# Regrouping a filter's DFT units beside the first batch of an MLP mixer: three places a step, and a thinner row of the second half

## The chip, the cores and the metric

The kernel runs on one core of a Trainium2 chip. The metric is the time of one execution in microseconds of that core. Engines: PE is TensorE, DVE is VectorE, ACT is ScalarE, POOL is GpSimd, SP is the queue that issues most loads. The granted clock (PEclk in the profiles) is the share of TensorE's full speed that was granted, as the profile records it; "half clock" below means matmuls that take up to twice as long where this figure is low: in the profile of the kernel before, two matmuls of L398 took 1.91 us at 355.92 (granted clock 0.50 from 356 to 359 us) and 1.02 us at 363.59 (1.00 from 360 to 370 us).

## The reference, cut to what matters

```python
# x: (8, 3008, 256) fp32
X = np.fft.rfft(x, axis=1)
Y = X * (filt_r + 1j * filt_i)[None]
x = np.fft.irfft(Y, n=3008, axis=1)                       # the filter
h = np.maximum(x.transpose(0, 2, 1) @ w_tok1, 0) @ w_tok2 # token mixing
u = x + h.transpose(0, 2, 1)
out = u + np.maximum(u @ w_ch1, 0) @ w_ch2                # channel mixing
```

The length 3008 is split as 64 x 47. For every batch the filter is 12 "length-64 units" (one matrix multiplication each) and, for a group of one or two batches, 32 "length-47 units" (a multiplication, the complex product with the filter on VectorE, and a multiplication back). A bank is the buffer in PSUM that such a multiplication writes; the next unit that uses the same bank has to wait until it has been read (for the length-64 units TensorE waited 16.7 us in all for this in the first profile of the kernel before).

## The kernel before

The batches go in the groups (0), (1, 2), (3, 4), (5, 6), (7). While the mixer works on one group, the filter of the next runs beside it, as a generator whose next step is called at fixed places of the mixer. Beside the first batch the last ten weights are converted too. (Code below is cut: `...` and missing arguments stand for what is left out.)

```python
def a_unit(b, c, tag):                      # length-64 unit
    ps = bank(tag)                          # beside the mixer: the one bank "b"
    nc.tensor.matmul(ps, wa, xs.pop((b, c))...)
    t1 = t1p.tile(...)
    nc.scalar.copy(out=t1, in_=ps)          # frees the bank
    nc.scalar.dma_start(z_d..., t1)

def dft(bs):
    ...
    for i, u in enumerate(todo):            # 24 length-64 units for two batches
        a_unit(*u, ("acc", "b")[i % 2] if first else "b")
        if i + XB < len(todo):
            x_load(*todo[i + XB])           # XB = 2: two x tiles
        yield
    ...
    load(0); load(1)
    yield
    yield
    for k in range(K2 + 1):                 # length-47 units, K2 = 32
        if k < K2:
            b_unit(k)                       # matmul to bank "b", four DVE operations
            ...
        if k >= 1:
            bi_unit(k - 1)                  # matmul to bank "acc", ACT copy
        yield
```

One step of the mixer (36 steps a batch: six blocks of rows, m, times six pairs of hidden tiles, jp); the yields are the places where the filter gets its turn:

```python
for i in range(n + 1):
    now, old = i < n, i >= 1
    next(convert, None)                     # first conversion: an ACT copy, five DVE operations
    if now:
        ...
        s = up_first(jp, ...)               # 8 matmuls, ACT copy
        up_middle(hhs[i], w, g, s)          # DVE
    one_step()                              # DVE: a piece of a finished block, or sums for the next
    if old:
        for f in h_sums(...): f()           # DVE
        down(mo, jo, 0, ...)                # 6 matmuls
    next(convert, None)                     # second conversion
    if now:
        up_last(jp, ...)                    # 6 matmuls, 2 DVE sums, 2 ACT relus
    one_step()
    loads()
    yield                                   # (1)
    if old:
        down(mo, jo, 1, ...)                # 8 matmuls
        if jo == JP - 1:
            todo_v.extend(finish(...))      # the block's finish: DVE
            one_step(); one_step()
    if now:
        if m + 1 < MT and jp in (3, 4):
            u_part(b, m + 1, jp - 3)        # token part: 12 matmuls, only in steps 3 and 4 of six
            ...
    loads()
    yield                                   # (2)
```

```python
for i, _ in enumerate(mix(b, next_ready, convert)):
    if not done and i % len(bs) == 0:       # first batch: at every yield; pairs: at (1)
        done = next(todo, "end") == "end"
```

## Time and profile before

| | |
|---|---|
| time, median | 2670.48 us (2663.97 to 2670.58, 3 runs) at first; 2668.18 us (4 runs) with the rounds of the change |
| first up-projection of the mixer | 202.31 us |
| second batch's first up-projection | 603.92 us |
| steps 0 to 4 (with conversions) | 75.47 us |
| steps 5 to 12 (rest of the length-64 units) | 67.83 us |
| steps 13 to 29 (length-47 units) | 195.17 us |

A step's start is read off TensorE's timeline: the first of the eight matmuls of line L492, the up-projection. Its length is the distance to the next one. How the page and the windows are read is shown in the prediction, on the lines themselves.

### The profile page before, as it was taken

How to read it: one execution, taken by the hardware profiler on the slowest of the kernel's cores; microseconds unless marked ns; L12 is line 12 of the kernel's file. 1: busy time of each engine (PE TensorE's matmuls, PEld its weight loads, DVE VectorE, ACT ScalarE, POOL GpSimd, SP SyncE). 2: the span in 40 equal slices, each digit the busy share in tenths (PEclk: the TensorE clock that was granted, in tenths of full speed). 3: DMA queues.
4: the chain of work that ended last, by engine and by line, in shares of the span. 5: the costliest groups of instructions: out<-in, count | busy, mean ns of one | idle time of the engine just before them, and what ended most of it. 6: DMA issues, size and time to landing. Idle time of an engine off the chain costs nothing.

```text
span 2667.9 us, 31511 instructions
## 1 busy us (share of the span) xinstructions
PE 2511.5 (94%) x10840; PEld 1997.6 (75%) x10840; DVE 1825.9 (68%) x3505; ACT 677.4 (25%) x1325; POOL 503.4 (19%) x926
## 2 busy tenths in 40 slices
PE   4666999999999999999999999999999999999997
PEld 1344766687787777788877777788888888888886
DVE  3886588846567688745658588755678586647675
ACT  2222322212322222212322122222222122212221
POOL 2324211111212111121121112121121111211221
PEclk8778999999999999999999999999999999999999
DMA  8663344322332222212233223211322211100000
GB/s 219 190 188 111 114 119 122 96 77 79 96 103 83 72 78 75 70 32 63 90 99 89 66 84 85 79 33 41 103 70 79 55 46 56 24 9 8 17 15 17
DMA packets 167158, 210.28 MB, mean 79 GB/s; under 512 B 35868, under 2 KB 115633, under 8 KB 166998
## 3 DMA queue, kind: packets, MB, share of 16 engines
q1 hardware_dynamic: 92937, 111.56, 14.4%
q0 software_dynamic: 30976, 44.53, 6.9%
q10 hardware_dynamic: 43085, 52.17, 6.0%
q8 instruction: 86, 1.41, 0.2%
q14 instruction: 74, 0.61, 0.1%
HBM read 133.15 MB, written 74.97 MB: 78 GB/s over the span
## 4 chain that ended last, share of the span: by engine, by line
PE 71%; DVE 16%; issue 2%; ACT 2%; DMA 0%; SPq 0%; DVEq 0%; POOL 0%; ACTq 0%; POOLq 0%
PE ps_po L526 24%; PE ps_pg L492 14%; PE ps_pg L508 11%; PE ps_acc L452 6%; PE ps_acc L435 5%; DVE t L470 3%; PE ps_acc L457 3%; DVE hh L470 3%; PE ps_b L382 2%; PE ps_b L349 2%; PE ps_acc L398 2%; DVE u L470 2%; DVE s L470 2%; DVE p L392 1%; DVE p L391 1%
## 5 line engine op out<-in xcount | busy, mean ns | idle before, releaser
L470 DVE TENSOR_TENSOR hh<-ps_pg,s 128x512 f32<-128x512 f32 (+3 forms) x864 | 482.6, 586 | 639.7 <-ACT s L495 639.7
L571 POOL DMA_DIRECT2D out_dram<-r x757 | 409.7, 550 | 1971.5 <-ACT hh L513 855.6
L513 ACT ACTIVATE hh<-hh 128x512 f32<-128x512 f32 (+1 forms) x576 | 347.9, 621 | 1141.6 <-DVE hh L470 1141.6
L526 PE MATMUL ps_po<-t,wc 128*128 128x256 f32 (+1 forms) x2304 | 535.8, 375 | 3.7 <-DVE t L470 2.4
L526 PEld LDWEIGHTS ps_po<-t,wc 128*128 128x128 f32 x2304 | 434.4, 190 | 128.3 <-issue 50.4
L492 PE MATMUL ps_pg<-v,wc 128*128 128x256 f32 (+1 forms) x1728 | 417.5, 378 | 1.5 <-DVE v L470 1.5
L526 PE MATMUL ps_po<-hh,wc 128*128 128x256 f32 (+1 forms) x1728 | 413.3, 375 | 3.1 <-ACT hh L513 3.1
L492 PEld LDWEIGHTS ps_pg<-v,wc 128*128 128x128 f32 x1728 | 330.5, 192 | 42.5 <-DVE v L470 1.9
L526 PEld LDWEIGHTS ps_po<-hh,wc 128*128 128x128 f32 x1728 | 328.2, 190 | 42.2 <-ACT hh L513 5.1
L508 PE MATMUL ps_pg<-u,wc 128*128 128x256 f32 (+1 forms) x1152 | 294.3, 378 | 16.0 <-DVE hh L470 15.7
L470 DVE TENSOR_TENSOR t<-t,hh 128x256 f32<-128x256 f32 (+1 forms) x576 | 243.5, 423 | 19.8
L508 PEld LDWEIGHTS ps_pg<-u,wc 128*128 128x128 f32 x1152 | 215.3, 190 | 52.8 <-DVE hh L470 28.6
L470 DVE TENSOR_TENSOR s<-ps_pg,hh 128x512 f32<-128x512 f32 (+1 forms) x288 | 196.1, 681 | 30.0
L452 PE MATMUL ps_acc<-w,h 128*128 128x512 f32 (+1 forms) x384 | 181.7, 596 | 15.8 <-ACT h L441 11.6
L470 DVE TENSOR_TENSOR t<-hh 128x512 f32<-128x512 f32 (+1 forms) x288 | 193.1, 671 | 0.6 <-ACT hh L513 0.6
L435 PE MATMUL ps_acc<-t,w 128*128 128x256 f32 x768 | 169.5, 383 | 6.3 <-DMA t<-g_tmp 5.0
L492 PE MATMUL ps_pg<-u,wc 128*128 128x256 f32 (+1 forms) x576 | 172.4, 381 | 0.4 <-DVE hh L470 0.4
L398 PE MATMUL ps_acc<-p,wi 128*96 128x512 f32 (+1 forms) x320 | 148.2, 546 | 23.7 <-DVE p L393 12.3
L508 PE MATMUL ps_pg<-v,wc 128*128 128x256 f32 (+1 forms) x576 | 169.2, 375 | 0.0
L435 PEld LDWEIGHTS ps_acc<-t,w 128*128 128x128 f32 x768 | 147.1, 192 | 28.1 <-issue 5.8
L382 PE MATMUL ps_b<-t,wb 96*128 96x512 f32 (+1 forms) x288 | 132.7, 542 | 23.2 <-DVE p L392 11.4
L495 ACT COPY s<-ps_pg 128x256 f32<-128x256 f32 (+1 forms) x288 | 105.8, 367 | 148.6 <-PE ps_pg L492 144.5
(67 smaller groups left out, 1947.5 us busy)
## 6 DMA issues: line engine op xcount, KB each, us to landing
z_tmp<-t ACTq DMA_DIRECT2D x96, 256.0 KB
t<-z_tmp SPq DMA_DIRECT2D x128, 192.0 KB
g_tmp<-t ACTq DMA_DIRECT2D x128, 192.0 KB
t<-g_tmp SPq DMA_DIRECT2D x48, 512.0 KB
x<-in_x_dram SPq DMA_DIRECT2D x184, 128.0 KB
out_dram<-r POOLq DMA_DIRECT2D x698, 32.0 KB, 1.8
wb<-wb_t SPq DMA_DIRECT2D x80, 96.0 KB
wi<-wi_t SPq DMA_DIRECT2D x80, 96.0 KB
```

The costliest lines, as they stand in the source:

```text
L382: nc.tensor.matmul(ps, wbs[k // WC][:, k % WC, :], t2s[k // KC][:, k % KC], start=True, stop=True)
L398: nc.tensor.matmul(ps[0:KR], wis[k // WC][:, k % WC, :], prods.pop(k), start=True, stop=True)
L435: nc.tensor.matmul(acc[:, t, :], w1[:, a, ts(t, P)], t4[b, a // TC4][:, a % TC4, :], start=(a == 0 and t == 0), stop=(a == A - 1 and t == ...
L452: nc.tensor.matmul(ps[:, 0:w], h1[:, t, ts(dh, P)], w2[:, t, ds(m * 512, w)], start=(t == 0), stop=False)
L457: nc.tensor.matmul(ps[:, ds(q * P, n)], t4[b, c][:, r, ts(dh, P)], wai[:, 0:n], start=False, stop=(q == 3))
L470: nc.vector.tensor_tensor(out=out, in0=in0, in1=in1, op=op)
L492: nc.tensor.matmul(ps[:, 0:hw], wc1[:, jp, n, :], mov, start=True, stop=True)
L495: nc.scalar.copy(out=s[:, 0], in_=g[0][:, 0, 0:hw])
L508: nc.tensor.matmul(ps[:, 0:hw], wc1[:, jp, n, :], mov, start=True, stop=True)
L513: nc.scalar.activation(out=hs, in_=hs, func=AF.Relu)
L526: nc.tensor.matmul(po[i][:, j, 0:hw], wc2[:, jp, n, :], mov, start=(jp == 0 and first == 1), stop=(jp == JP - 1 and last == 1))
L571: q.dma_start(rows[g, e, :, ds(h * A + 4 * m, n)], blocks[ts(g, CW), h, e, 0:n])
```

## The change

The intent: in the first batch's early steps TensorE idles (23.5 of 75.5 us), so give it more length-64 units there (three a step instead of two), and use the steps that this frees to take the length-47 units less densely, because VectorE is nearly full beside them (85% busy).

```diff
@@ dft
-            yield
+            yield i + 1 < len(todo)          # true until the last length-64 unit
@@ mix
                 down(mo, jo, 0, ...)
+            yield i, 0
             next(convert, None)
...
-            yield
+            yield i, 1
...
-            yield
+            yield i, 2
@@ the loop over the groups
+            spread = True
...
-                for i, _ in enumerate(mix(b, next_ready, convert)):
-                    if not done and i % len(bs) == 0:
-                        done = next(todo, "end") == "end"
+                for i, place in mix(b, next_ready, convert):
+                    if not done and (place == 1 or bs == GROUPS[0] and (spread or place == 2 and i % 3)):
+                        spread = next(todo, "end")
+                        done = spread == "end"
```

For the other groups the calls stay where they were: at place 1 of each step.

Two words for what follows. Places 0, 1 and 2 of a step are its three yields; the place of a step *in six* is its number modulo six, which is jp (step 17 is at place 5 of six). "The spread" is the second half of the change, the length-47 units taken less densely; the variable `spread` in the code is true until it begins.

## The prediction

> **What bounds the kernel now.** I read the page first, then windows cut at the stages of the first batch, then that stretch's timelines of TensorE, VectorE and ScalarE, then its waits.
>
> ```profile
> PE 2511.5 (94%) x10840; PEld 1997.6 (75%) x10840; DVE 1825.9 (68%) x3505; ACT 677.4 (25%) x1325; POOL 503.4 (19%) x926
> ...
> PE   4666999999999999999999999999999999999997
> ```
>
> TensorE is busy from the fourth slice (200 us) to the end, so its queue sets the time. The first 200 us (first group's filter, alone) are not touched. The change acts only beside the first batch of the mixer, from the first up-projection at 202.31 us to the second batch's at 603.92. I cut that stretch where TensorE's timeline shows the stages change:
>
> ```profile
> core 0: us, PE busy (x) PEld busy (x) DVE busy (x) ACT busy (x) POOL busy (x), PEclk, DMA share, GB/s
> 202.31:277.78 75.47, 51.94 (x172) 34.61 (x171) 52.40 (x91) 20.12 (x37) 31.04 (x53) 0.89 0.33 102
> 277.78:345.61 67.83, 66.66 (x278) 50.83 (x277) 38.12 (x73) 22.20 (x42) 8.73 (x16) 1.00 0.43 136
> 345.61:540.78 195.17, 181.21 (x677) 123.80 (x676) 166.64 (x286) 47.87 (x92) 25.98 (x48) 0.97 0.37 105
> 540.78:603.92 63.14, 61.55 (x303) 55.45 (x302) 28.80 (x60) 11.72 (x25) 8.65 (x16) 1.00 0.26 82
> ```
>
> Row 1 is mixer steps 0 to 4, beside which the last ten weight conversions run (two a step): TensorE is idle for 23.5 of 75.5 us. Row 2 is steps 5 to 12, with the rest of the 24 length-64 units at two a step: 1.2 us idle. Row 3 is steps 13 to 29, with the 32 length-47 units, two a step: 14.0 us idle, VectorE at 85%. Row 4 has no filter work. So the whole idle time that any regrouping here can win is 40 us, 1.5% of the time; 2% can't come from it.
>
> In row 1 TensorE isn't the bound. Its long waits are for a length-64 unit's bank, which ScalarE frees late:
>
> ```profile
> 214.67 1.12 PE L349 MATMUL ps_b<-x,wa 128*128 128x512 f32 x2 [2.66 <-ACT t L351]
> ...
> 230.74 2.08 PE L349 MATMUL ps_b<-x,wa 128*128 128x512 f32 x2 [5.21 <-ACT t L351]
> ...
> 245.85 1.40 PE L349 MATMUL ps_b<-x,wa 128*128 128x512 f32 x2 [3.55 <-ACT t L351]
> ```
>
> That copy (L351) stands in ScalarE's queue behind the relus, and these behind VectorE's conversions. VectorE in turn waits for ScalarE's first conversion copy of the next step:
>
> ```profile
> 217.68 0.43 DVE L220 TENSOR_SCALAR top<-top 128x512 uint32<-128x512 uint32 x1 [4.20 <-ACT top L219]
> ...
> 234.70 0.43 DVE L220 TENSOR_SCALAR top<-top 128x512 uint32<-128x512 uint32 x1 [5.15 <-ACT top L219]
> ```
>
> The loop of a step is therefore: relu, copy of the unit after the up-projection, the unit at the step's end on TensorE, its copy, its store's issue, conversion copy, some 11 us of VectorE work, relu. TensorE has slack beside it.
>
> In row 3 TensorE waits for VectorE to finish reading the one bank of the length-47 products:
>
> ```profile
> 497.21 1.12 PE L382 MATMUL ps_b<-t,wb 96*128 96x512 f32 x2 [1.78 <-DVE p L392]
> ```
>
> [...] ScalarE takes the conversion copy at 216.99 only after the two unit copies and the store's issue at 216.45.[...] after the 2.23 us stall at 354.90 the granted clock of 350 to 360 is 0.83, but after the 1.78 us stall at 497.21 it stays 1.00.[...] the four operations of a length-47 unit take 684, 693, 684 and 693 ns, 2.75 us in all.[...] x loads and z stores there never fill a stage (share 0.33 and 0.43).
>
> **The change part by part.** No instruction is added or removed; units move. Units per plain step on TensorE: 6.04 us mixer (step 12, with no unit), 0.86 a length-64 unit (two 512-column matmuls, 6.90 minus 6.04 in the second batch), 0.86 each for the two halves of a length-47 unit, 2.6 for the token part (L452 1.72 plus L457 0.89) in two steps of six.
>
> *Length-64 units.* Three places a step: 24 units take steps 0 to 7 instead of 0 to 11. The new place is after the first part of the down-projection, ahead of the second conversion. In steps 0 to 4 it puts five more units, 5 x 0.86 = 4.3 us, into TensorE's slack; the other steps lose as much. Does it lengthen the loop? The new unit's copy (0.58) and store issue (0.35) come ahead of the second conversion copy (0.67) on ScalarE. For step 1: down-projection ends near 220.5, unit 221.4, copy 222.0, issue 222.4, conversion copy 223.1; VectorE asks for it at 224.7. Step 2: 240.2 against 240.33. So it fits, with nothing to spare in one step: 0. In steps 5 to 7 bank b must be free between the new place and the next: six matmuls (1.29) against a copy of 0.6: it fits. The stalls of about 0.28 at the step's end occur in three steps instead of five (5, 7, 8, 11 and the one at 338.60): 0.6 gained. Sum: 4.9 us off. The x data of the third unit must arrive within one unit, 1.29, one unit and 1.73 of matmuls, 3.9 us after the first; at 286.28 a load is issued and its burst ends near 289.2, 3.0 us. It fits narrowly.
>
> *Length-47 units.* They start at step 9 and take 5 places in 3 steps, ending at step 29 as before (the last call is at step 29's middle instead of its end). The second place is left out in every third step: 0 and 3 of each six. Step lengths of before, by place in six (steps 23 to 28): 11.25, 9.91, 12.78, 11.10, 11.88, 11.88 (the last two 12.14 in the earlier, wider blocks). By work alone a plain step with two units is 9.5, so stalls are at 5, 1 and 2. At place 3, 1.73 of pure work goes: 10.4. At place 0 the same goes: 7.8. At place 1 the VectorE queue decides: the finish of a block (2.2 us) and the two products must pass. I run it through with the durations above: without the product of place 0's end, VectorE is ready for the next step at 487.2 instead of 489.95, the step begins at 484.1, its second product's bank is freed 7.2 us later (as at 347.64 to 354.84) at 494.4, so the step is 12.3, still stalled. Places 2 and 5 keep their queues: 11.1 and 11.25. So the stalls stay, and the units now spend stalls in one more step (11). Steps 8 to 29: 6.0+9.5+12.1+11.25, then twice 7.8+12.3+11.1+10.4+12.1+11.25, then 7.8+12.3+11.1+10.4+11.2+6.0 = 227.6. Steps 0 to 7: 75.5+9.1+8.7+9.1 = 102.4. Total 330.0; before it is 540.78-202.31 = 338.5. That is 8.5 us off if no stall drops the clock. Before, such drops cost: steps 13, 14, 17, 19, 20 are longer than their work and idle time by some 5 us in all. As the stalls remain, I let 3 us of that come back: 5.5 us off. 2670.5 - 5.5 = 2665.
>
> **The rivals.** (1) The spread really frees VectorE (85% busy over 17 steps becomes about 80% over 21), and the stalls at 1, 2 and 5 vanish: all 14 us idle and 5 us of clock come back with the 4.9: some 20 us off, 2650. For it: the stalls are VectorE's. Against: the two places that lose a unit are not those that stall. (2) The third unit lengthens the conversion loop: its copy and issue delay the second conversion copy by up to 0.9 us in five steps, 4.6 us, which eats the gain: 2670. For it: 240.2 against 240.33. Against: the slack in steps 1, 3 and 4, over a microsecond. (3) A transfer comes late: the x loads at three a step, or the first products' data, now loaded from step 8. The first product needs the last z store to land (2.3 us at 340.38) and a load; there is one plain step between, as before. Worth 1 us a step in steps 5 to 7 at most, 2668. (4) The second batch's token sums wait for the filter: the filter ends half a step earlier than before, so no.
>
> **Range and chances.** The centre is 2665. Three runs of before spread from 2664 to 2670.6, so 3 us of scatter goes on the 5 of my working: 2655 to 2671. Faster by over 2% would need 53 us, more than all idle time there is: 0.01. Slower by over 2% needs a loop broken that I have not seen: 0.01. Within 2%: 0.98.
>
> **What would show it.** Right: the first five steps last 75 to 76 us with more TensorE work and less idle time; the twelve steps before the products become eight; step 7 ends near 305; products stall TensorE for as long as before in all (12 to 17 us), at places 1, 2 and 5 of six; the second batch starts near 598 instead of 603.9, and everything after it is shifted only. Wrong: a first stage over 78 us, with longer waits of VectorE for the conversion copy (rival 2); product stalls under 6 us and a second batch at 585 (rival 1); waits for x or z at L349 and L382 (rival 3); a difference that arises after the second batch's start.

## The result

The changed kernel takes 2663.53 us (median of 4, 2660.95 to 2664.48) against 2668.18 us (4 runs). The ratio is 0.9983 with an interval of 0.9965 to 1.0: within 2%, and hardly clear of no difference. The predicted time was 2665.

The windows of the changed kernel, cut at the same stages as those of before (steps 0 to 4, the remaining length-64 units in steps 5 to 7, steps 8 to 29 with the length-47 units, the rest of the batch); the columns are in the first line:

```profile
core 0: us, PE busy (x) PEld busy (x) DVE busy (x) ACT busy (x) POOL busy (x), PEclk, DMA share, GB/s
200.53:279.78 79.25, 58.40 (x183) 38.55 (x181) 53.62 (x91) 23.69 (x42) 33.95 (x57) 0.85 0.41 130
279.78:306.90 27.12, 26.55 (x103) 19.18 (x102) 16.39 (x32) 10.10 (x19) 0.00 (x0) 1.00 0.55 179
306.90:534.96 228.06, 212.52 (x841) 151.53 (x840) 187.80 (x324) 57.39 (x109) 34.71 (x64) 1.00 0.35 102
534.96:597.74 62.78, 61.55 (x303) 55.64 (x302) 29.34 (x62) 11.83 (x25) 8.65 (x16) 1.00 0.20 67
```

The batch takes 397.2 us instead of 401.6, 4.4 less. The first stage got longer (79.25 against 75.47); everything between it and step 30 takes 255.2 us instead of 263.0. VectorE's share in the third row, which now holds 22 steps instead of 17, fell from 85% to 82%, but TensorE's idle time there did not fall: 15.5 us against 14.0.

TensorE's own waits over the whole first batch say the same. Before, then after (what waited, for what, us in total, times, longest):

```profile
PE ps_b L349 <- ACT t L351: 16.7, 9, 5.2
PE ps_b L382 <- DVE p L392: 11.4, 8, 2.2
PE ps_pg L508 <- DVE hh L470: 8.6, 8, 2.3
```

```profile
PE ps_b L349 <- ACT t L351: 17.7, 5, 5.2
PE ps_b L382 <- DVE p L392: 14.0, 9, 1.8
PE ps_pg L508 <- DVE hh L470: 1.6, 5, 0.5
```

The stalls of the products (L382) are nine instead of eight and longer in sum. (A second profile of before, below, has nine too, 12.1 us in all, but two of those are of 0.15 us; here all nine are over 1.3.) What went away is most of the third row: 6.5 of its 8.6 us lay in the five conversion steps, as waits of `up_last` for VectorE, in whose place a length-64 unit now runs; 0.7 us of that is left. The first row loses its four short waits of steps 5 and later, and keeps the five long ones, one for each conversion step.

### The profile page after: what moved, and what is told of

Same layout as the page of the kernel before. It is cut to its first block, busy times and chain, and to the rows that moved or that the text cites. A ratio compares the mean times of both kernels' runs of the same rounds, so it can differ in the third digit from the quotient of the medians.

```text
span 2662.7 us, 31542 instructions
## 1 busy us (share of the span) xinstructions
PE 2509.5 (94%) x10840; PEld 2000.5 (75%) x10840; DVE 1827.1 (69%) x3505; ACT 678.4 (25%) x1325; POOL 503.4 (19%) x926
## 4 chain that ended last, share of the span: by engine, by line
PE 73%; DVE 18%; DMA 3%; issue 3%; ACT 2%; POOL 0%; SPq 0%; ACTq 0%; DVEq 0%; POOLq 0%
PE ps_po L526 25%; PE ps_pg L492 15%; PE ps_pg L508 11%; PE ps_acc L452 6%; PE ps_acc L435 5%; DVE t L470 3%; PE ps_acc L457 3%; DVE hh L470 3%; PE ps_b L382 3%; PE ps_b L349 3%; PE ps_acc L398 2%; DVE u L470 2%; DVE s L470 2%; DMA x<-in_x_dram 1%; DVE p L392 1%
## 5 line engine op out<-in xcount | busy, mean ns | idle before, releaser
L398 PE MATMUL ps_acc<-p,wi 128*96 128x512 f32 (+1 forms) x320 | 145.4, 537 | 26.5 <-DVE p L393 14.8
L382 PE MATMUL ps_b<-t,wb 96*128 96x512 f32 (+1 forms) x288 | 133.2, 545 | 21.9 <-DVE p L392 14.0
```

The lines of the kernel that those rows point to most:

```text
L382: nc.tensor.matmul(ps, wbs[k // WC][:, k % WC, :], t2s[k // KC][:, k % KC], start=True, stop=True)
L398: nc.tensor.matmul(ps[0:KR], wis[k // WC][:, k % WC, :], prods.pop(k), start=True, stop=True)
```

## The experiments

Eight runs were made, one of the kernel before and seven of variants. All gave correct results. The first four ran on one chip, the last four on another, each set with its own rounds of the kernel before (medians 2667.72 and 2666.99 us, 7 runs each). Differences of 3 us are at the edge of what these times tell, so the verdicts rest mainly on stage lengths of the profiles, which repeat to 0.1 us where no stall and no clock drop is involved (steps 30 to 35 took 63.14 and 63.13 us in the two profiles of before).

### The kernel before, once more

No edit.

> The kernel before, unchanged, for a second profile. My theory: the drops of the clock behind the stalls of steps 13, 14, 17, 19 and 20 (some 5 us in the first profile)[...] need not come again; then steps 13 to 29 take 190 us instead of 195.2, and the first five steps 75 to 77 us. Rival: the drops belong to the spacing of the units, and steps 13 to 29 take 194 to 196 us again. Time 2664 to 2671 either way.

Measured: 2667.23 us, ratio 0.9996 (0.9982 to 1.0011). Its windows:

```profile
198.26:275.75 77.49, 48.66 (x173) 32.49 (x172) 53.73 (x91) 20.15 (x37) 34.24 (x57) 0.93 0.33 100
275.75:343.57 67.82, 66.65 (x277) 50.82 (x276) 38.10 (x73) 22.20 (x42) 8.76 (x16) 1.00 0.43 136
343.57:536.47 192.90, 178.11 (x678) 122.08 (x677) 166.36 (x286) 47.80 (x92) 26.03 (x48) 0.99 0.37 107
```

Two things follow. Steps 13 to 29 took 192.9 us, between the two expectations: step 13 stalled for 2.22 us, as in the first profile (2.23), but lasted 11.12 instead of 12.01 us, and step 17 lost 1.2 us of excess, while step 19 was as long again (14.0). The granted clock around the stall of step 13 (350 to 360 us in both profiles) is 1.00 here and was 0.83 there. The same stall is thus followed by a clock drop in one execution and not in the next, but they don't all vanish. And the first stage scatters by 2 us without any change: step 0 took 15.55 us here and 13.32 in the first profile. The mixer began 4 us earlier here and then waited 2.41 us, by the profile for a weight of GpSimd's; the first profile has a wait of 1.52 us there, put down to VectorE. That time is lost or won before the change begins to matter.

### Length-64 units as in the change, length-47 units as before

```diff
-... (spread or place == 2 and i % 3)
+... (spread or place == 2)
```

> Length-64 units at three places as in the change, length-47 units at two places in every step as before. My theory: the gain is in the length-64 units, the spread is worth about 1 us: first up-projection to step 8 takes 105 to 107 us as in the changed kernel, the stalls of the products sum to 12 to 16 us, and the time is within 2 us of the changed kernel (2662 to 2666). Rival, the spread is the gain: the time is that of the kernel before (2666 to 2670).

Measured: 2663.05 us, ratio 0.9983 (0.9968 to 0.9998), the same ratio as the full change.

```profile
201.25:279.63 78.38, 53.28 (x182) 34.32 (x181) 53.58 (x91) 23.57 (x42) 33.46 (x56) 0.93 0.44 132
279.63:308.02 28.39, 26.54 (x103) 19.13 (x102) 16.39 (x32) 10.11 (x19) 0.00 (x0) 1.00 0.53 173
308.02:535.20 227.18, 212.62 (x841) 150.92 (x840) 187.77 (x325) 57.71 (x110) 34.79 (x64) 1.00 0.40 118
```

The third row covers steps 8 to 29 as in the changed kernel: 227.2 us against 228.1 with the spread. So the spread is worth nothing here, and the gain comes from the length-64 units. The batch took 396.5 us. The first up-projection to step 8 took 106.8 us, as expected; the stalls of the products summed to 11.0 us in nine, under the 12 to 16 expected, but waits of `up_last` for VectorE in the same steps were 3.0 us instead of 0.9.

### The second place left out elsewhere

```diff
-... (spread or place == 2 and i % 3)
+... (spread or place == 2 and i % 6 not in (1, 5))
```

> As the changed kernel, but the second place is left out at steps 1 and 5 of each six instead of 0 and 3: as many units over as many steps. My theory: a stall comes where VectorE's queue (finish of a block, sums of the next) is longest in a step without token part, so this choice removes the stalls of steps 1 and 5; six steps take about 61 us instead of 64.9, 9 to 11 us less in all: 2652 to 2655. Rival, VectorE's mean load counts: the same 2663 as the changed kernel.

Measured: 2658.53 us, ratio 0.996 (0.9945 to 0.9975). That is less than the changed kernel's time; the intervals of the two ratios overlap, but steps 5 to 29 took 252.1 us, against 255.2 and 256.1 in the two profiles with the change's layout (the other is the run with the new place later, below). So which steps are thinned matters and rival "mean load" falls, but the gain is about half of what I expected. Steps 17 to 22 took 62.7 us (64.9 in the changed kernel, 61 expected), at a granted clock of 1.00: the stalls of step 5 went, but step 1 kept 0.97 us, now as a wait of `up_last`, and the stall of step 2 grew from 1.35 to 1.69.

```profile
421.57 1.13 PE L508 MATMUL ps_pg<-u,wc 128*128 128x256 f32 x4 [0.97 <-DVE hh L470]
```

The sixes before and after (steps 11 to 16 and 23 to 28) also lost time at half clock, some 3 us in steps 15, 26 and 27: their granted clock is 0.97, and 1.00 in the changed kernel's profile. Behind the stall of step 14:

```profile
371.77 1.13 PE L382 MATMUL ps_b<-t,wb 96*128 96x512 f32 x2 [1.69 <-DVE p L392]
372.73 1.25 PE L398 MATMUL ps_acc<-p,wi 128*96 128x512 f32 x2
373.77 1.06 PE L492 MATMUL ps_pg<-u,wc 128*128 128x256 f32 x2
374.63 2.54 PE L492 MATMUL ps_pg<-v,wc 128*128 128x256 f32 x6
```

In an undisturbed step the last line's six matmuls take 1.46 us and the two before them 0.59. From 374 to 378 us the granted clock is 0.65. The same stall of 1.69 us in step 20 was followed by no drop.

### No length-64 unit at the end of the conversion steps

```diff
-... (spread or place == 2 and i % 3)
+... (spread and (i > 4 or place == 0) or not spread and place == 2 and i % 3)
```

> As the changed kernel, but in the five steps with conversions no length-64 unit at the step's end. My theory: that unit and its copy and store stand in the loop that bounds these steps, 2 to 3 us a step, so the first five steps take 68 to 71 us instead of 79; the five units cost 4.3 us later; together 2656 to 2660. Rival: the five steps are bound by VectorE's own work and the weights' loads; they stay at 76 to 79 us and the time rises to 2666 to 2668.

Measured: 2660.03 us, ratio 0.9971 (0.9954 to 0.9987). The first stage is where it was expected, the time at the upper end:

```profile
201.35:269.99 68.64, 50.84 (x173) 34.02 (x172) 53.47 (x91) 20.53 (x37) 33.47 (x56) 0.90 0.38 119
```

VectorE's waits for the conversion copy, in the changed kernel's first stage and in this one:

```profile
DVE top L220 <- ACT top L219: 20.4, 5, 5.1
```

```profile
DVE top L220 <- ACT top L219: 10.9, 5, 2.7
```

So the loop is as described: the unit at the step's end, its copy and its store stood between the relu and the next conversion. It cost 10.6 us in five steps. That it is the place and not the number of units, the kernel before shows: with as many units in these steps as here (two a step), one of them at the step's end, it took 75.5 and 77.5 us. The five units then cost 6.0 us later in steps 5 to 29 (261.2 us instead of 255.2) and 2.2 in steps 30 to 35 (64.9 instead of 62.8), together 3.9 more than their own 4.3, since the length-47 units now run on into steps 30 and 31 and stall once more in step 29. So 2.4 us of the batch are left of the 10.6.

### The new place behind the second conversion

```diff
-            yield i, 0
             next(convert, None)
+            yield i, 0
             if now:
                 up_last(...)
```

> As the changed kernel, but the new place is behind the second conversion, so that on ScalarE the conversion copy goes ahead of the new unit's copy and store. Mine: in the changed kernel the new unit held the second conversion copy up in step 0 (1 us wait of VectorE) and hardly later, so the first five steps go from 79.2 to 77.5-78.5 us and the time stays within 2 us of 2663. Rival (2) of the prediction in full: the first five steps fall to 75 us, the time to 2659.

Measured: 2664.3 us, ratio 0.999 (0.9976 to 1.0005); the first stage took 79.09 us. The time is as expected; the stage is not. In step 0 what I expected did happen. In the changed kernel ScalarE takes the new unit's copy first:

```profile
207.59 0.58 ACT L351 COPY t<-ps_b 128x512 f32<-128x512 f32 x1 [2.40 <-PE ps_b L349]
208.21 0.36 ACTq L352 DMA_DIRECT2D z_tmp<-t  x1
208.75 0.68 ACT L219 ACTIVATE top<-st 128x512 f32<-128x512 f32 x1 [0.57 <-ACT t L351]
```

and VectorE waits for the conversion copy that comes behind it:

```profile
209.47 0.43 DVE L220 TENSOR_SCALAR top<-top 128x512 uint32<-128x512 uint32 x1 [0.98 <-ACT top L219]
```

This wait of step 0 is 0.98, 0.75 and 0.63 us in the three profiles with the new place ahead of the conversion (the changed kernel and the two runs with the same first stage), and absent in this run and in both profiles of before; step 0 took 14.98 us here, 1.4 less than in the changed kernel. Steps 2 and 3 gave most of it back, 15.11 and 17.31 us against 14.60 and 16.54, because their last unit, which stands in the loop, ran at half clock (2.08 and 2.07 us, against 1.57 and 1.31 in the changed kernel). The end of step 2, first in this run, then in the second profile of before:

```profile
246.37 2.08 PE L349 MATMUL ps_b<-x,wa 128*128 128x512 f32 x2 [3.54 <-ACT t L351]
```

```profile
244.08 1.13 PE L349 MATMUL ps_b<-x,wa 128*128 128x512 f32 x2 [3.54 <-ACT t L351]
```

The wait in brackets is the same 3.54 us, the unit takes 0.95 us more. The granted clock there is 0.62 (245.5 to 250 us) and 1.00 (243 to 247.5). So in the first stage a microsecond a step comes and goes with the clock, and one profile of a kernel can't show a gain of one.

### The conversion's copy one conversion earlier

On top of the run without units at the end of the conversion steps, each conversion is cut behind its ScalarE copy, and the copy of the next is issued with the present one, so ahead of the relus:

```diff
         nc.scalar.activation(out=top, in_=hi_f, func=AF.Copy, scale=2.0 ** -112)
+        if late:
+            yield
@@ weights()
             next(s, None)
+            if n <= i + 1 < len(steps):
+                next(steps[i + 1])
             load(not n - 2 <= i < n)
```

(The four callers say `yield from rounded(...)`.)

> As the run without length-64 units at the end of the five conversion steps, and each conversion's copy on ScalarE is issued one conversion earlier, ahead of the relus. Mine: the loop through ScalarE is then gone and VectorE's own 11 us a step bound the first five steps: 57 to 61 us instead of 68.6, the time 2649 to 2654. Rival: the weights' loads or GpSimd's sums bound them, 66 to 69 us, and the time stays at 2660.

Measured: 2650.59 us, ratio 0.994 (0.9924 to 0.9957). The first stage:

```profile
199.93:257.36 57.43, 46.91 (x172) 32.54 (x171) 54.39 (x91) 18.38 (x34) 34.52 (x53) 0.94 0.47 143
```

VectorE is busy for 54.4 of 57.4 us and waits for ScalarE only once, 1.9 us, at the start. The conversion steps are now bound by VectorE's own work. Whether the earlier copy alone would do, with the units left at the steps' ends, was not tried.

### The two together, and three length-47 units beside the token part

```diff
-not spread and place == 2 and i % 3
+not spread and place == 2 and i % 6 not in (1, 5)
```

> The former with the second length-47 place left out at steps 1 and 5 of six. Mine: the two gains add, since they lie in different stages: 3 to 6 us under the former, 2644 to 2650. Rival: the stalls only move on, within 2 us of the former.

Measured: 2644.14 us, ratio 0.9916 (0.9901 to 0.9931); 6.9 us less in the first batch (377.1 against 384.0). The two gains add; that is 6.5 us in the time, a little over the 3 to 6 expected.

```diff
-not spread and place == 2 and i % 6 not in (1, 5)
+not spread and (place == 2 or place == 0 and i > 10) and i % 6 in (3, 4)
```

> As the former, but three length-47 units in each step with a token part (3 and 4 of six) and one in every other, again ten in six steps. Mine: the steps without a token part then hardly stall; the two with one take 14.5 to 15.5 us with a stall of about 1 us at their second unit; six steps take 60 to 62 us; the time is 0 to 5 us under the former, 2640 to 2650. Rival: three units in a step overfill VectorE's queue, the steps take over 17 us and the time rises by 3 to 8 us.

Measured: 2640.35 us (2640.16 to 2642.25), ratio 0.9901 (0.9887 to 0.9916). This version beats both kernels: 27 us under the kernel before, 1.0%. Against the run just above it is 3.8 us in the medians, with overlapping intervals; the profiled executions don't show it in the time (2642.25 and 2641.78 us, in the former's the mixer began 4.4 us earlier), but steps 5 to 29 took 251.4 us instead of 254.8. Steps 3 and 4 of six, which have the token part's 2.6 us on TensorE, take the three units in 15.2 and 14.8 us, with one stall each. In step 21:

```profile
413.94 1.02 PE L385 MATMUL ps_b<-t,wb 96*128 96x512 f32 x2
...
418.18 1.12 PE L385 MATMUL ps_b<-t,wb 96*128 96x512 f32 x2 [1.05 <-DVE p L395]
...
424.33 1.02 PE L385 MATMUL ps_b<-t,wb 96*128 96x512 f32 x2
```

(The edit above moved the lines: L385 is L382 of the other kernels, L395 is L392.) The other four steps take 7.8 to 8.6 us. Six steps sum to 62.0 us against 64.9 in the changed kernel, as many units in each. TensorE's waits for the products over the batch are

```profile
PE ps_b L385 <- DVE p L395: 5.1, 6, 1.1
```

against 14.0 us in nine waits.

## Why the prediction was right or wrong, point by point

**That 2% can't come from here: right.** The stretch had 40 us of idle TensorE time. Even the best version wins 27. The bound is not as strict as it was put, since idle time leaves out what is lost at half clock: in steps 0 to 4 the same number of matmuls kept TensorE busy for 51.9 us before, at a granted clock of 0.89, and for 46.9 in the run with the earlier copy, at 0.94. With these 5 us and the 5 named for the length-47 steps it would be about 50, still under the 53 that 2% asks.

**Length-64 units in steps 5 to 7: right.** 26.9 us predicted, 27.1 measured. The x loads fit narrowly, as said: one wait of 0.45 us, in step 7. One count was wrong: the kernel before has four short stalls at the ends of steps (5, 7, 8 and 11), not five, since the one at 338.60 is that of step 11.

**"It fits, with nothing to spare in one step: 0" for the conversion loop: wrong by a small amount.** I had checked steps 1 and 2. In step 0 the up-projection starts late and the new unit's copy held the conversion up by 0.98 us. The first stage took 79.25 us instead of the predicted 75.5. Of the 3.8 us, 2.2 are the scatter of step 0 that the second profile of before shows too (15.55 against 13.32, with the same wait of 2.4 us in both long cases), 1.0 is this wait, and the remaining 0.5 or so is left to the clock: the units at the ends of steps 2 and 3 ran slower (1.57 and 1.31 us; the same unit of step 2 took 1.13 in the second profile of before), at a granted clock of 0.67 and 0.68 (246 to 251 and 263 to 268 us). The split is an estimate; no run separates the three.

**Length-47 units: right, step by step.** 227.6 us were predicted for steps 8 to 29, without clock drops, and 228.1 measured. By place in six, from steps 17 to 22 (predicted in brackets): 11.30 (11.25), 7.76 (7.8), 12.18 (12.3), 11.10 (11.1), 10.37 (10.4), 12.15 (12.1). The stalls stayed, and one was added.

**The 3 us of clock drops: wrong.** In the changed kernel's profile the granted clock of this stretch is 1.00 and no step is longer than its work and stall. So the sum of 8.5 us, less 3 for the clock, was the wrong way to a nearly right number: the clock gave back its 3 us and the first stage took 3.8. That the two misses nearly cancel is luck. The batch shrank by 4.4 us.

**Rival 1 (the spread frees VectorE): refuted.** Without the spread the time and the batch are the same, or 0.8 us better. The two places that lose a unit are not those that stall, which was the argument against it; where the second place is dropped at two of the stalling steps instead, 3.6 us of the batch go.

**Rival 2 (the new unit lengthens the conversion loop): present, at about a fifth of its size.** Up to 4.6 us were named, 1.0 was found, in one step. Its sign did come up as the prediction wrote it: the first stage took over 78 us, and VectorE waited longer for the conversion copy. In the first profile of before these waits were

```profile
DVE top L220 <- ACT top L219: 17.9, 4, 5.1
```

and 18.6 us in the second, against 20.4 in the changed kernel. But the run with the new place behind the conversion, where the new copy can't hold it up, waits 20.3 us as well and takes 79.1 us, so the sign doesn't single this rival out. All four profiles with three units in these steps (78.4 to 79.3 us) are longer than both of before (75.5 and 77.5); what of that is scatter was not settled.

**Rival 3 (late transfers): 0.45 us** in the changed kernel, at the x loads, but it varies: 1.5 us in the run with the new place later, and 0.5 in the one without the spread, where a unit also waited 1.3 us for what the profile takes for a filter load. Up to 1 us a step was named. The two issues of one x tile (256 KB) took about 0.5 and 0.6 us in the kernel before, of the 3.0 us from the first issue at 286.28 to the end of the burst near 289.2. **Rival 4: no**, the token sums started without a wait.

**"Everything after it is shifted only": nearly.** The second batch starts at 597.74 us (598 predicted). What follows takes 2065.0 us against 2064.0 and 2063.9 in the two profiles of before. This microsecond, spread over the second, third and fifth batch, stays unexplained; in the other runs the same stretch takes 2063.9 to 2065.7 us.

What stays open besides: when a stall is followed by half clock. The same 2.2 us of step 13 were followed by it in one execution (granted clock 0.83 from 350 to 360 us) and not in another (1.00), and of two stalls of 1.69 us in one profile, steps 14 and 20 of the run with places 1 and 5 left out, only the first was (0.65 from 374 to 378 us). It was not settled by an edit.

## What to carry to other kernels

When an engine idles beside another's loop, ask first whether the work you move there enters that loop through a queue that both use: here ScalarE took the conversion copy at 208.75 only behind the unit's copy at 207.59 and its store's issue at 208.21, the units' place at the step's end cost VectorE ten microseconds of waiting, and the extra units at the new place cost about one. Taking the unit at the step's end out shortened the five steps from 79.3 to 68.6 us, and issuing the next conversion copy earlier in the queue to 57.4. Ask also in which steps to thin work: here it won nothing at places 0 and 3 of six, 3.6 us of the batch at 1 and 5, and most when the units went to the two steps in which TensorE has most work of its own. And run a queue through by hand with the trace's durations: that gave the changed kernel's step lengths to about 0.1 us, while the mean share of a busy engine said nothing. It has limits: for the layout without places 1 and 5, 61 us were expected for six steps, and they took 62.7.
